# Moving the small softmax-sum transfers from SyncE's queue to ScalarE's, with other due times in the planner that orders an attention stage

## The chip, the cores and the metric

The kernel runs on one core of a Trainium2 chip. The metric is the device time of one execution in microseconds, as the median of several runs.

## The reference

Three blocks follow each other, all in 32-bit floats. q is averaged over pairs of rows first.

```python
# attention: 4 batches, 8 heads, 1152 keys, 576 pooled queries, head size 64
q_pool = q.reshape(B, H, S // 2, 2, D).mean(axis=3)
scores = scale * np.matmul(q_pool, k.transpose(0, 1, 3, 2))
scores = scores - np.max(scores, axis=-1, keepdims=True)
attn = np.exp(scores)
attn = attn / (np.sum(attn, axis=-1, keepdims=True) + 1e-09)
x = np.matmul(attn, v)                  # -> 2304 tokens x 512
# soft mixture of experts: 8 experts, 4 slots each, 512 -> 1024 -> 512
logits = x @ phi                        # softmax over tokens (d) and over slots (c)
slot_input = d.T @ x
slot_out[e] = np.maximum(slot_input[e] @ w1[e], 0.0) @ w2[e]
y = c @ slot_out
# gated block, 512 -> 2048 -> 512
h = y @ w_in
out = (h * np.cos(h)) @ w_out
```

## The kernel before

**The attention stage** works on 16 pairs of heads. A pair has two halves (`a`) of 288 queries, and a half has nine key tiles (`t`) of 128 keys. For each key tile `scores` (L457, L460) makes a 128x576 block on TensorE in PSUM, `exps` (L468) turns it into `E` on ScalarE, `e_sum` (L479, L481) adds `E` into a running sum `ES` on GpSimd, and `av` (L487) multiplies `E` by V on TensorE into a sum of its own in PSUM. `av` splits TensorE's array by columns, while scores split it by rows; the planner calls these modes "c64" and "r64".

Ahead of a half, `max_pair` (L412, TensorE) and `max_pair_red` (L421, VectorE) find the maxima that the scores are shifted by: 9 such blocks for the first half, 6 for the second. Scores, maxima, transposes and the spread sums share three PSUM slots (`take="2"`): a slot is free again only when ScalarE or VectorE has read it. `E` has five buffers.

After a pair, `fin` closes it: `sum4` adds `ES` over partitions (L508), `sum4_copy` moves it to SBUF, **`sum4_turn`** (L520) sends 4.5 KB by DMA into a layout of 128 partitions (`rt`), `sum4_rec` takes reciprocals as a high and a low part (`hl`, L548 to L551), **`sum4_back`** (L557) sends the two parts back by two DMAs (`rh`), `sum4_spread` (L565) broadcasts them on TensorE, and `pair_mul` (L570) multiplies.

Beside this, 32 pieces of w_in and w_out are converted (`conv_load` to `conv_store`: ScalarE L289 and L294, VectorE L298, L301 and L307, GpSimd L313) and stored to DRAM, and expert weights are loaded ahead into buffers as they come free (`late_piece`, `held_piece`, L251). The tiles `raw` and `cvt` of the conversion are two such buffers, which take two pieces of 256 KB each once the last conversion is done.

**The planner** `in_order` sets the order of all this. Each operation has an engine, an assumed time, what it depends on, a PSUM or `E` slot and a due time; the planner walks through an assumed time line and takes, per engine, the operation with the earliest due time among those that can start. A change of TensorE's mode counts as 2.5 us of due time. Each engine then runs its list strictly in that order. `GROUPS` says which key tiles' `av` form one operation; `PAIR`, `MAX_BEG`, `AV_DUE` and the 13.6 in `convert` set due times.

**The last pair** (p = 15) is finished in finer steps: `fin_sum` (L530), `rec_mul` (L541 to L577), `l_x` (L793), `l_mm` (L782), `l_max`, `l_exp`, `l_weigh`. The first half's are planned too; the second half's are written out behind the planner's list, beginning with an `l_mm`, `l_eT` (L744) and a `fin_sum`.

**Behind attention** come the experts (L1175, L1208), which read 128 weight pieces of 256 KB, then the converted weights are loaded back (L1251 to L1259), and then the gated block (L1343, L1379, L1381) runs to the end.

Of the kernel before, what the change touches and what calls it, by code (L numbers as in the profile page):

```python
# [45 lines left out]
LAT = {"PE": 0.27, "ACT": 0.1, "DVE": 0.1, "POOL": 0.12, "SP": 0.0}  # L46
# [1 line left out]
KB_US = 250.0  # L48
PAIR = 26
FIRST_AT = 22.0  # L50
MAX_BEG, MAX_MID, MAX_END = 4, 6, 4
AV_DUE = 6
GROUPS = ((0, 1), (2, 3), (4, 5), (6, 7, 8))
LAST_GROUPS = ((0, 1), (2, 3), (4, 5), (6, 7))


class Op:


    def __init__(self, steps, fn, deps=(), due=0.0, take=None, mode=None, port=False, kb=None, at=0.0):  # L60
        self.steps, self.fn, self.deps = steps, fn, [d for d in deps if d is not None]
        self.due, self.take, self.mode, self.port, self.kb, self.at = due, take, mode, port, kb, at
        self.after, self.users, self.of = [], 0, []
        self.end = None

# [8 lines left out]
def in_order(ops, room):  # L74

    left = {}
    for o in ops:
        left[o] = len(o.deps)
        for d in o.deps:
            d.after.append(o)  # L80
    ready = [o for o in ops if not left[o]]
    free = {e: 0.0 for e in ("PE", "ACT", "DVE", "POOL", "SP")}
    spots = {k: [(0.0, i) for i in range(n)] for k, n in room.items()}
    mode, done, until, wire = None, 0, {}, 0.0
    while ready:
        best = {}
        for o in ready:
            e = o.steps[0][0]
            t = max(free[e], o.at, max((d.end + (1.0 if e == "SP" else 0.0) if d.steps[-1][0] != e or d.kb else d.end - LAT[e] for d in o.deps), default=0.0))
            if o.take:  # L90
                if not spots[o.take]:
                    continue
                t = max(t, min(spots[o.take])[0])
            if o.port:
                t = max(t, free["POOL" if e == "DVE" else "DVE"] if until.get("POOL" if e == "DVE" else "DVE") else 0.0)
            best.setdefault(e, []).append((t, o))
        pick = None
        for e, c in best.items():
            t0 = min(t for t, _ in c)
            near = [(o.due + (2.5 if o.mode and o.mode != mode else 0.0) + 0 * (t - t0), t, o) for t, o in c if t <= t0 + 0.1]  # L100
            due, t, o = min(near, key=lambda x: x[0])
            if pick is None or t < pick[0]:
                pick = t, o
        t, o = pick
        ready.remove(o)
        spot = None
        if o.take:
            spot = min(spots[o.take])
            spots[o.take].remove(spot)
            o.spot, o.free_at = spot[1], 0.0  # L110
        for e, dur in o.steps:
            t = max(t, free[e])
            if e == "PE" and o.mode != mode:
                t += SWITCH[o.mode]
                mode = o.mode
            free[e] = t + dur
            until[e] = o.port
            t = t + dur + LAT[e]
        if o.kb is not None:

            wire = max(wire, t) + o.kb / KB_US
            t = wire + 2.5
        o.end = t
        o.fn(o)
        done += 1
        if o.take and not o.users:
            spots[o.take].append((o.end, o.spot))
        for x in o.of:
            x.users -= 1
            x.free_at = max(x.free_at, o.end)  # L130
            if not x.users:
                spots[x.take].append((x.free_at, x.spot))
        for a in o.after:
            left[a] -= 1
            if not left[a]:
                ready.append(a)
    assert done == len(ops), (done, len(ops))
# [3 lines left out]
def kernel(  # L141
# [12 lines left out]
    nc = tc.nc  # L154
# [6 lines left out]
    NP = B * H // 2  # L161
# [339 lines left out]
    fs = {}  # L501
# [15 lines left out]

    def sum4_turn(p):
        rt = sm.tile([128, HF // 32], FP32, tag="rt", name="rt")
        nc.sync.dma_start(out=rt, in_=fs.pop("r").rearrange("(r x) (j c) -> r x j c", x=32, j=32)[:, 0])  # L520
        fs["rt"] = rt


# [30 lines left out]
    def sum4_back(p):  # L554
        hl = fs.pop("hl")
        for i in range(2):
            nc.sync.dma_start(  # L557
                out=rh[4 * i:4 * i + 4].bitcast(FP32).rearrange("r (j c) -> r j c", j=32), in_=hl[:, i].bitcast(FP32)
            )

# [246 lines left out]
    def due_at(p, a=0, t=0):  # L807
        return FIRST_AT + (p + (a * NJ + t) / (2 * NJ)) * PAIR

    def attention():  # L810
        ops = []

        def add(steps, f, *args, **kw):
            def fn(o):
                cur[0] = o
                f(*args)

            o = Op([steps] if isinstance(steps[0], str) else steps, fn, **kw)
            ops.append(o)
            return o  # L820
# [69 lines left out]
                    out_[p, a] = add(("ACT", .32), av_out, p, a, deps=[avo[p, a, NJ - 1], mul.get(p - 2)], due=due_at(p, a, 10)).uses(first)  # L890

        def fin(p):
            z = due_at(p + 1)
            s4[p] = m = add(("PE", .5), sum4, p, deps=[es[p, 0, NJ - 1], es[p, 1, NJ - 1], spread.get(p - 1)], due=z + 4, take="1", mode="c32")
            c = add(("ACT", .31), sum4_copy, p, deps=[m], due=z + 5).uses(m)
            c = add(("SP", .6), sum4_turn, p, deps=[c], due=z + 5.2, kb=50)
            c = add([("DVE", .13), ("ACT", .12), ("DVE", .12)], sum4_rec, p, deps=[c], due=z + 9)
            c = add(("SP", 1.2), sum4_back, p, deps=[c], due=z + 10, kb=100)
            spread[p] = m = add(("PE", .55), sum4_spread, p, deps=[c], due=z + 14, take="2", mode="r64")
            b = (p - HP - 1) // HP  # L900
            mul[p] = add(("DVE", .66), pair_mul, p, deps=[m, out_[p, 1], bl.get(b), *[bx.get((b, g)) for g in range(5)]], due=z + 15).uses(m)
            if p % HP == HP - 1 and p < NP - 1:
                b = p // HP
                bl[b] = add([("PE", 1.2), ("DVE", .5), ("ACT", .4), ("DVE", .4)], b_logits, b, deps=[mul[p], bp1.get(b - 1)], due=z + 19, take="1", mode="c32")
                for g in range(5):
                    bx[b, g] = add([("PE", .45), ("ACT", .55)], b_x, b, g, deps=[mul[p], bp1.get(b - 1)], due=z + 20 + 3 * g, take="2", mode="r64")
                e = add([("PE", .27), ("ACT", .35)], b_e, b, deps=[bl[b]], due=z + 24, take="1", mode="full")
                bp0[b] = add(
                    [("PE", .9), ("DVE", .1), ("ACT", .2), ("DVE", 1.5)], b_part, b, 0, deps=[e, *[bx[b, g] for g in range(4)]],
                    due=z + 34, take="1", mode="c32",  # L910
                )
                bp1[b] = add([("PE", .9), ("ACT", .55)], b_part, b, 1, deps=[bp0[b], bx[b, 4]], due=z + 36, take="1", mode="c32")

        def convert(i):
            z = FIRST_AT + 8 + i * 13.6
            if i and i - 1 not in cu:
                return
            l = add(("SP", .6), conv_load, i, deps=[cu[i - 1]["sign"]] if i else (), due=z - 9, kb=512, at=z - 12)
            x = add(("ACT", .62), conv_act, i, deps=[l, cu[i - 1]["store"] if i else None], due=z)
            y = add(("ACT", .62), conv_low, i, deps=[x], due=z + .5)  # L920
            m = add(("DVE", .8), conv_mag, i, deps=[x], due=z + 2, port=True)
            s = add(("DVE", .65), conv_sign, i, deps=[m], due=z + 3, port=True)
            r = add(("POOL", 1.25), conv_round, i, deps=[s, y], due=z + 5, port=True)
            cu[i] = dict(sign=s, store=add(("SP", .5), conv_store, i, deps=[r], due=z + 6, kb=256))
# [13 lines left out]
        for i in range(RING):  # L938
            z = due_at(3.4 + i * 8 / 36)
# [4 lines left out]
        p, b = NP - 1, B - 2  # L944

        def d(t):
            return due_at(p, 1, t)

        def maxima():
            for i in range(3):  # L950
# [43 lines left out]
        c = add(("DVE", .35), lambda: l_max(lt[0], 0), deps=[m], due=d(6.5)).uses(m)  # L994
        c = add([("DVE", .1), ("ACT", .75)], lambda: l_exp(lt[0], 0), deps=[c], due=d(7)).uses(m)
# [4 lines left out]
    with tc.manual_schedule():  # L1000
# [8 lines left out]
        for h in range(2):  # L1009
# [6 lines left out]
            out=pick, in0=idn[0:64, 0:4].rearrange("p (r o) -> p r o", o=1).to_broadcast([64, 4, 64]),  # L1016
# [3 lines left out]
            out=sel.rearrange("p (s o) -> p s o", o=1), in_=idn.rearrange("p (g s) -> p s g", g=4), axis=AX.X, op=ALU.add  # L1020
# [9 lines left out]
        p = NP - 1  # L1030
# [40 lines left out]
        for kk in range(HP):  # L1071
            nc.tensor.matmul(
                out=pm[:, kk * NS:(kk + 1) * NS], lhsT=part[0][:, kk * 128:(kk + 1) * 128], rhs=sel, start=True, stop=True
# [96 lines left out]
        for g in range(NG):  # L1170
            h1p = [ps_m.tile([128, 512], FP32, tag=f"h{a}", name=f"h{a}") for a in range(2)]
            for kk in range(HP):
                for a in range(2):
                    for e in range(4):
                        nc.tensor.matmul(  # L1175
                            out=h1p[a][32 * e:32 * e + 32, :], lhsT=slT[:, kk, :], rhs=pieces[used + e],
# [298 lines left out]
```

## Time and profile before

| what | us |
|---|---|
| three runs | 836.56 median (834.33 to 836.94) |
| the profiled execution | 832.92, of it 831.1 span from first to last instruction |
| attention's pairs until the last exponential | about 0 to 521.7 of the span |
| the rest of attention's list and the last pair's close | 521.7 to 549.6 |
| experts | 549.6 to 594.3 |
| gated block with its start | 594.3 to 831.1 |

The last four rows are marked off by instructions in the trace: the last `exps` ends near 521.7, the first expert matmul starts at 549.6, the last one's sum is done by 594.3. The profiled execution lies 3.6 us under the median of the three runs.

### The profile page before, as it was taken

The page shows a single profiled execution, that of the slowest core. Times are in us where ns is not written, and L with a number is a line of the kernel's source. Part 1 is how long each engine was busy: PE and PEld are TensorE (multiplying, and loading weights), DVE is VectorE, ACT ScalarE, POOL GpSimd, SP SyncE. Part 2 cuts the span into 40 slices and gives each one's busy share as a digit, 9 for nine tenths or more (in the row PEclk, how much of TensorE's full clock was granted, in tenths as well). Part 3 has the DMA queues.
Part 4 walks back from the last instruction along what each step waited for, and adds up shares of the span by engine and source line. Part 5 has one row for each costly group of instructions (what it writes and reads, how often), then busy time and mean ns, then how long its engine had stood idle before and what let it go on. Part 6 is the DMA issues. An engine that isn't in the chain of part 4 may idle for free.

```text
span 831.1 us, 16390 instructions
## 1 busy us (share of the span) xinstructions
PE 776.5 (93%) x6336; PEld 531.1 (64%) x6336; DVE 555.2 (67%) x828; ACT 448.7 (54%) x837; POOL 536.2 (65%) x415
## 2 busy tenths in 40 slices
PE   4999999999999999989999999699999999999997
PEld 2766666666666666556665656333467888888886
DVE  6777877777877767868876775522276756666662
ACT  1565556465555564555665655223376766666662
POOL 1698889787798877878876979411375544444442
PEclk9999999999999999999999999999999999999999
DMA  8432553553634654443515314299951000000001
GB/s 201 122 96 69 148 137 128 141 167 124 161 116 113 190 156 147 126 144 107 126 42 158 130 58 141 97 328 386 386 205 26 26 5 22 27 26 26 26 26 26
DMA packets 86482, 101.48 MB, mean 122 GB/s; under 512 B 48260, under 2 KB 48260, under 8 KB 86404
## 3 DMA queue, kind: packets, MB, share of 16 engines
q1 hardware_dynamic: 86324, 100.30, 40.2%
q8 instruction: 50, 0.82, 0.4%
q14 instruction: 28, 0.23, 0.1%
q10 hardware_dynamic: 80, 0.13, 0.0%
HBM read 87.10 MB, written 13.11 MB: 121 GB/s over the span
## 4 chain that ended last, share of the span: by engine, by line
PE 69%; DVE 16%; ACT 6%; issue 4%; POOL 3%; DMA 1%; ACTq 0%; SPq 0%; POOLq 0%; DVEq 0%
PE o L1379 15%; PE av L487 13%; PE mx L457 11%; PE o L1381 7%; DVE nm L421 6%; PE mx L412 5%; PE mx L460 3%; POOL ES L481 2%; PE po L1208 2%; ACT E L468 2%; PE h L1175 2%; DVE cvt L298 2%; PE u L1343 2%; DVE cvt L301 2%; DVE cvt L307 2%
## 5 line engine op out<-in xcount | busy, mean ns | idle before, releaser
L481 POOL TENSOR_TENSOR ES<-ES,E 128x576 f32<-128x576 f32 x223 | 325.9, 1462 | 45.0 <-ACT E L468 31.4
L421 DVE TENSOR_REDUCE nm<-mx 128x2 f32<-128x768 f32 x240 | 223.8, 953 | 81.2 <-PE mx L412 80.2
L468 ACT ACTIVATE E<-mx 128x576 f32<-128x576 f32 x288 | 179.5, 650 | 145.5 <-PE mx L460 126.9
L457 PE MATMUL mx<-Q,kX 64*128 64x288 f32 x1152 | 178.8, 322 | 14.1 <-DVE nm L421 9.8
L487 PE MATMUL av<-E,vn 128*64 128x288 f32 x1152 | 169.8, 421 | 0.0
L1363 POOL TENSOR_TENSOR lo<-g,hi 128x512 fp32r<-128x512 f32 (+1 forms) x73 | 94.2, 1291 | 110.5 <-DVE hi L1361 105.8
L457 PEld LDWEIGHTS mx<-Q,kX 64*128 64x128 f32 x1152 | 111.0, 186 | 66.0 <-DVE nm L421 25.6
L1379 PE MATMUL o<-w_hi,hi 128*128 128x512 f32 x288 | 113.2, 393 | 0.7 <-DVE hi L1361 0.7
L1381 PE MATMUL o<-w_lo,hi 128*128 128x512 f32 x288 | 113.2, 393 | 0.3 <-DVE w_lo L1267 0.3
L487 PEld LDWEIGHTS av<-E,vn 128*64 128x64 f32 x1152 | 72.2, 137 | 55.7 <-issue 23.0
L412 PE MATMUL mx<-kX,Q 64*128 64x384 f32 x480 | 92.4, 403 | 9.7 <-DVE nm L421 4.4
L457 PE MATMUL mx<-Q,kY 64*128 64x288 f32 x576 | 87.7, 294 | 0.0
L460 PE MATMUL mx<-NM,one_row 64*128 64x288 f32 x576 | 87.4, 293 | 0.0
L1379 PE MATMUL o<-w_hi,lo 128*128 128x512 f32 x288 | 77.4, 389 | 0.0
L479 POOL TENSOR_TENSOR ES<-E 128x576 f32<-128x576 f32 x31 | 45.8, 1477 | 46.1 <-ACT E L468 46.1
L1348 ACT ACTIVATE t<-u 128x512 f32<-128x512 f32 (+1 forms) x73 | 43.0, 591 | 58.0 <-PE u L1343 58.0
L1350 DVE SCALAR_TENSOR_TENSOR r<-t,u 128x512 f32<-128x512 f32 (+1 forms) x73 | 49.4, 679 | 36.4 <-ACT t L1348 35.8
L1359 DVE SCALAR_TENSOR_TENSOR g<-r,u 128x512 f32<-128x512 f32 (+1 forms) x73 | 49.6, 680 | 35.4 <-ACT r L1357 35.4
L412 PEld LDWEIGHTS mx<-kX,Q 64*128 64x128 f32 x480 | 45.5, 191 | 38.6 <-DVE nm L421 15.0
L313 POOL TENSOR_TENSOR cvt<-cvt 128x512 uint32<-128x512 uint32 x32 | 44.2, 1381 | 31.7 <-DVE cvt L307 16.6
L1379 PEld LDWEIGHTS o<-w_hi,lo 128*128 128x128 f32 x288 | 54.1, 188 | 11.4
L1379 PEld LDWEIGHTS o<-w_hi,hi 128*128 128x128 f32 x288 | 54.2, 188 | 10.9 <-DVE hi L1361 0.9
(223 smaller groups left out, 1007.0 us busy)
## 6 DMA issues: line engine op xcount, KB each, us to landing
w<-in_moe_w_dram SPq DMA_DIRECT2D x89, 256.0 KB
qn<-in_q_dram SPq DMA_DIRECT2D x16, 576.0 KB
kn<-in_k_dram SPq DMA_DIRECT2D x16, 576.0 KB
vn<-in_v_dram SPq DMA_DIRECT2D x16, 576.0 KB
raw<-in_moe_w_in_dram SPq DMA_DIRECT2D x16, 512.0 KB
w<-cvt SPq DMA_DIRECT2D x32, 256.0 KB
raw<-in_moe_w_out_dram SPq DMA_DIRECT2D x16, 512.0 KB
lw<-in_moe_w_dram SPq DMA_DIRECT2D x29, 256.0 KB
```

What stands on the lines that cost most here:

```text
L412: nc.tensor.matmul(out=m[:, h, 0:384], lhsT=Q1[p % 2][hs, AT[i]:AT[i] + 128], rhs=X[p][hs, ks], start=True, stop=True)
L421: nc.vector.tensor_reduce(out=nm3[p][:, i, :, c:c + 1], in_=m[:, :, 0:384], axis=AX.X, op=ALU.max)
L457: nc.tensor.matmul(out=sc[:, h, 0:HF], lhsT=x[hs, ks], rhs=y[hs, qs], start=(n == 0), stop=False)
L460: nc.tensor.matmul(out=sc[:, h, 0:HF], lhsT=one_row[hs, :], rhs=NM[p % 2][hs, qs], start=False, stop=True)
L468: nc.scalar.activation(out=e, in_=sc[:, :, 0:HF], func=AF.Exp, scale=1.0 / 16.0)
L481: nc.gpsimd.tensor_tensor(out=ES[p, a], in0=ES[p, a], in1=E[p, a, t], op=ALU.add)
L487: nc.tensor.matmul(out=av_t[p, a][64 * h:64 * h + 64, 0:HF], lhsT=vn[p][:, h, t, :], rhs=E[p, a, t][:, h, :], start=(t == 0), stop=(t == N ...
L1350: nc.vector.scalar_tensor_tensor(out=r, in0=t, scalar=MAGIC, in1=u, op0=ALU.subtract, op1=ALU.subtract)
L1359: nc.vector.scalar_tensor_tensor(out=g, in0=r, scalar=1.0, in1=u, op0=ALU.subtract, op1=ALU.mult)
L1363: nc.gpsimd.tensor_tensor(out=lo[:, 0:n], in0=g, in1=hi[:, 0:n].bitcast(FP32), op=ALU.subtract)
L1379: nc.tensor.matmul(out=o, lhsT=x, rhs=w_hi[ff], start=(ff == 0 and not part), stop=bool(part and ff == NF - 1))
L1381: nc.tensor.matmul(out=o, lhsT=x, rhs=w_lo[ff], start=False, stop=False)
```

## The change

`sum4_turn` and `sum4_back` are issued in ScalarE's queue instead of SyncE's. The planner counts ScalarE as taken for 0.65 and 1.2 us by them, and the data as landed 2.8 us later (`land`). Each key tile's `av` is an operation of its own, due 5.1 us behind its scores instead of 8.7 (`AV_DUE` times 26/18). The conversions are due every 11.5 us instead of 13.6. The first half's maxima become due 6 us later (`MAX_BEG` 4 to 10). `fin` of pair 14 and the planned close of pair 15 are due 8 us sooner (`SOON`). Among operations that start within 0.1 us of each other, a later start now counts five times against the due time.

```diff
-MAX_BEG, MAX_MID, MAX_END = 4, 6, 4
-AV_DUE = 6
-GROUPS = ((0, 1), (2, 3), (4, 5), (6, 7, 8))
-LAST_GROUPS = ((0, 1), (2, 3), (4, 5), (6, 7))
+MAX_BEG, MAX_MID, MAX_END = 10, 6, 4
+AV_DUE = 3.5
+CONV, SOON = 11.5, 8
+GROUPS = tuple((i,) for i in range(9))
+LAST_GROUPS = GROUPS[:8]
...
-            near = [(o.due + (2.5 if o.mode and o.mode != mode else 0.0) + 0 * (t - t0), t, o) for t, o in c if t <= t0 + 0.1]
+            near = [(o.due + (2.5 if o.mode and o.mode != mode else 0.0) + 5 * (t - t0), t, o) for t, o in c if t <= t0 + 0.1]
...
-        o.end = t
+        o.end = t + o.land
...
-        nc.sync.dma_start(out=rt, in_=fs.pop("r").rearrange("(r x) (j c) -> r x j c", x=32, j=32)[:, 0])
+        nc.scalar.dma_start(out=rt, in_=fs.pop("r").rearrange("(r x) (j c) -> r x j c", x=32, j=32)[:, 0])
...
-            nc.sync.dma_start(
+            nc.scalar.dma_start(
...
-            z = due_at(p + 1)
+            z = due_at(p + 1) - (SOON if p == NP - 2 else 0)
...
-            c = add(("SP", .6), sum4_turn, p, deps=[c], due=z + 5.2, kb=50)
+            c = add(("ACT", .65), sum4_turn, p, deps=[c], due=z + 5.2, land=2.8)
...
-            c = add(("SP", 1.2), sum4_back, p, deps=[c], due=z + 10, kb=100)
+            c = add(("ACT", 1.2), sum4_back, p, deps=[c], due=z + 10, land=2.8)
...
-            z = FIRST_AT + 8 + i * 13.6
+            z = FIRST_AT + 8 + i * CONV
...
-            return due_at(p, 1, t)
+            return due_at(p, 1, t) - SOON
```

What the change moves is seen at three places. A new line near the top shifts all later line numbers by one.

TensorE, second half of pair 7, from its fifth key tile on; L487/L488 is `av`, where x4 is two key tiles and x2 is one (two heads each). Before:

```order
L457 MATMUL mx<-Q_1_110,kX 128x288 x2
L457 MATMUL mx<-Q_1_110,kY 128x288 x2
L457 MATMUL mx<-Q_1_112,kX 128x288 x2
L460 MATMUL mx<-NM_114,one_row 128x288 x2
L412 MATMUL mx<-kX,Q_0_109 128x384 x2
L487 MATMUL av<-E,vn 64x288 x4
L565 MATMUL mx<-rh,pick 128x288 x2
```

After, about the same place:

```order
L461 MATMUL mx<-NM_114,one_row 128x288 x2
L488 MATMUL av<-E,vn 64x288 x2
L413 MATMUL mx<-kX,Q_0_109 128x384 x2
...
L461 MATMUL mx<-NM_114,one_row 128x288 x2
L413 MATMUL mx<-kX,Q_0_109 128x384 x2
L488 MATMUL av<-E,vn 64x288 x2
L413 MATMUL mx<-kX,Q_0_109 128x384 x2
L488 MATMUL av<-E,vn 64x288 x2
```

Where the old list has one run of two key tiles, the new one often has a run of a single tile, with a maximum between two of them. Over the whole program the list has 127 runs of `av` before (93 of two tiles, 31 of three, 3 of other lengths up to five) and 174 after (85 of one tile, 73 of two, 9 of three, 5 of four, 2 of five).

TensorE, the end of the planner's list, where L793 is `l_x`, L782 `l_mm`, L565 the spread of pair 14's sums and L457/L460 the last scores. Before:

```order
L460 MATMUL mx<-NM_114,one_row 128x288 x2
L487 MATMUL av<-E,vn 64x288 x4
L565 MATMUL mx<-rh,pick 128x288 x2
L487 MATMUL av<-E,vn 64x288 x8
L793 MATMUL mx<-idn,xT 96x128 x8
L782 MATMUL mx<-xT,phi_sb 32x288 x4
L793 MATMUL mx<-idn,xT 96x128 x4
L729 MATMUL mx<-nM_124,gsel 128x1
L782 MATMUL mx<-xT,phi_sb 32x288
L744 MATMUL mx<-idn,e_7217 96x32 x3
```

After (the spread stands further ahead, at the start of the second half):

```order
L488 MATMUL av<-E,vn 64x288 x10
L794 MATMUL mx<-idn,xT 96x128 x4
...
L783 MATMUL mx<-xT,phi_sb 32x288 x4
L794 MATMUL mx<-idn,xT 96x128 x4
...
L461 MATMUL mx<-NM_114,one_row 128x288 x2
L794 MATMUL mx<-idn,xT 96x128 x4
L488 MATMUL av<-E,vn 64x288 x2
L730 MATMUL mx<-nM_124,gsel 128x1
L488 MATMUL av<-E,vn 64x288 x4
L783 MATMUL mx<-xT,phi_sb 32x288
L745 MATMUL mx<-idn,e_7215 96x32 x3
```

Before, the spread, two `l_x` and the `l_mm` of four products, the third `l_x` and six tiles of `av` stood behind the last scores; now one `l_x` and three tiles of `av` do.

SyncE's queue at the same place, where L317 is the store of a converted piece, lw the pieces that go into freed buffers (nine of them into kX, kY, vn, Q1, Q2 and NM), hw others of that kind. Before:

```order
L282 DMA raw<-in_moe_w_out_dram 128x1024
...
L317 DMA w_31_160<-cvt 128x512
L251 DMA lw<-in_moe_w_dram 128x512 x11
L251 DMA hw<-in_moe_w_dram 128x512 x8
L251 DMA w<-in_moe_w_dram 128x512 x49
L1251 DMA win_q<-w_0_129 128x512
```

After:

```order
L252 DMA hw<-in_moe_w_dram 128x512 x2
L252 DMA lw<-in_moe_w_dram 128x512 x9
L252 DMA hw<-in_moe_w_dram 128x512 x8
L252 DMA w<-in_moe_w_dram 128x512 x49
L1252 DMA win_q<-w_0_129 128x512
```

The last four conversions have left the end of the list. Counted by the scores ahead of them, conversion 31 stood behind the last scores and now stands in the middle of pair 14, and the four pieces for `raw` and `cvt` are issued there too.

## Rows read from the trace of the kernel before

**Rows 1.** Stretch: length, busy of PE, PEld, DVE, ACT, POOL, clock, DMA share, GB/s.

```profile
24.20:500.40 476.20, 451.09 (x4548) 298.93 (x4548) 361.65 (x471) 269.20 (x499) 387.68 (x268) 0.99 0.45 127
...
521.70:549.60 27.90, 19.11 (x130) 9.64 (x126) 16.21 (x39) 8.27 (x21) 7.13 (x6) 0.94 0.41 133
549.60:594.30 44.70, 44.30 (x300) 13.22 (x300) 8.85 (x46) 10.35 (x32) 9.58 (x29) 1.00 1.05 386
594.30:612.90 18.60, 16.95 (x104) 11.69 (x104) 10.12 (x20) 13.15 (x29) 10.45 (x9) 1.00 1.05 386
```

**Rows 2.** The same view for two pair periods (first exponential to the next pair's).

```profile
239.40:268.20 28.80, 28.38 (x287) 19.25 (x287) 20.75 (x29) 17.11 (x32) 25.05 (x18) 1.00 0.57 155
335.00:368.30 33.30, 29.06 (x285) 18.93 (x284) 27.01 (x31) 16.98 (x31) 28.53 (x21) 1.00 0.45 121
```

**Rows 3.** Waits from 24.2 to 500.4: total us, times, longest.

```profile
ACT E L468 <- PE mx L460: 122.7, 128, 2.9
...
PEld mx L457 <- DVE nm L421: 25.6, 43, 2.5
...
PE mx L457 <- DVE nm L421: 9.8, 16, 2.2
```

**Rows 4.** TensorE's timeline in pair 2, around one run of `av`.

```profile
72.43 0.34 PE L412 MATMUL mx<-kX,Q 64*128 64x384 f32 x2
72.70 1.19 PE L487 MATMUL av<-E,vn 128*64 128x288 f32 x8
73.83 0.40 PE L457 MATMUL mx<-Q,kX 64*128 64x288 f32 x2
74.06 0.29 PE L457 MATMUL mx<-Q,kY 64*128 64x288 f32 x2
74.19 0.29 PE L457 MATMUL mx<-Q,kX 64*128 64x288 f32 x2
...
74.46 0.33 PE L412 MATMUL mx<-kX,Q 64*128 64x384 f32 x2
74.63 0.29 PE L457 MATMUL mx<-Q,kX 64*128 64x288 f32 x2
```

**Rows 5.** The chain that ended last: `av` of two and three tiles.

```profile
34.42 1.12 PE av L487 x8
38.23 1.61 PE av L487 x12
```

**Rows 6.** The small transfer `rt` around pair 1's beginning: ns min/median/max, start.

```profile
L520 SPq DMA_DIRECT2D rt<-rec x1: 705/705/705, 57.3 to 57.3; - x1
L548 DVE RECIPROCAL rt<-rt x1: 205/205/205, 61.5 to 61.5; 128x9 f32<-128x9 f32 x1
...
  DVE rt L548: 0.9, 1
```

**Rows 7.** The issues of `rh` on SyncE, ns min/median/max.

```profile
L557 SPq DMA_DIRECT2D rh<-hl x30: 547/580/1177, 61.9 to 514.2; - x30
```

**Rows 8.** TensorE's timeline from the last scores to the last pair's close.

```profile
515.77 0.71 PE L530 MATMUL mx<-ES,ones 128*64 128x288 f32 x4 [1.92 <-POOL ES L481]
...
519.49 0.29 PE L460 MATMUL mx<-NM,one_row 64*128 64x288 f32 x2
...
529.11 1.09 PE L793 MATMUL mx<-idn,xT 128*96 128x128 f32 x4 [5.20 <-DVE xT L577]
...
530.74 2.99 PE L782 MATMUL mx<-xT,phi_sb 128*32 128x288 f32 x8
533.66 0.64 PE L793 MATMUL mx<-idn,xT 128*96 128x128 f32 x4
...
536.84 0.67 PE L782 MATMUL mx<-xT,phi_sb 128*32 128x288 f32 x2
```

**Rows 9.** SyncE's queue there: start, us, issue.

```profile
543.50 5.49 SPq L251 DMA_DIRECT2D lw<-in_moe_w_dram  x11
```

**Rows 10.** Busy times just ahead of the experts, columns as in rows 1.

```profile
543.00:549.60 6.60, 6.05 (x59) 3.50 (x59) 1.99 (x9) 3.12 (x9) 0.00 (x0) 1.00 0.79 244
```

More of the change, by code (lines that the diff above doesn't have):

```diff
@@ L50, with __init__ @@
 FIRST_AT = 22.0
-MAX_BEG, MAX_MID, MAX_END = 4, 6, 4
-AV_DUE = 6
-GROUPS = ((0, 1), (2, 3), (4, 5), (6, 7, 8))
-LAST_GROUPS = ((0, 1), (2, 3), (4, 5), (6, 7))
+MAX_BEG, MAX_MID, MAX_END = 10, 6, 4
[3 more added lines that the diff above has]
+LAST_GROUPS = GROUPS[:8]
 class Op:
-    def __init__(self, steps, fn, deps=(), due=0.0, take=None, mode=None, port=False, kb=None, at=0.0):
+    def __init__(self, steps, fn, deps=(), due=0.0, take=None, mode=None, port=False, kb=None, land=0.0, at=0.0):
         self.steps, self.fn, self.deps = steps, fn, [d for d in deps if d is not None]
-        self.due, self.take, self.mode, self.port, self.kb, self.at = due, take, mode, port, kb, at
+        self.due, self.take, self.mode, self.port, self.kb, self.land, self.at = due, take, mode, port, kb, land, at
         self.after, self.users, self.of = [], 0, []
@@ L88, in in_order @@
             e = o.steps[0][0]
-            t = max(free[e], o.at, max((d.end + (1.0 if e == "SP" else 0.0) if d.steps[-1][0] != e or d.kb else d.end - LAT[e] for d in o.deps), default=0.0))
+            t = max(free[e], o.at, max((d.end + (1.0 if e == "SP" else 0.0) if d.steps[-1][0] != e or d.kb or d.land else d.end - LAT[e] for d in o.deps), default=0.0))
             if o.take:
```

## The prediction

> **What bounds the kernel now.** I read the busy times by stretch first [rows 1]. Attention's pairs take 476 of 831 us, and TensorE is busy in 451 of them; but matmuls overlap, so this share hides short stalls. No other engine is near: GpSimd 388, VectorE 362, ScalarE 269 us. Behind the pairs stands a stretch of 27.9 us with TensorE busy in only 19.1. The experts' stretch and the one behind it run at 386 GB/s with the DMA share full: there the weights set the pace. What follows them holds nothing that the change touches.
>
> Then I compared pair periods [rows 2]. The same TensorE instructions (287 and 285 matmul records) take 28.8 us in one pair and 33.3 in another. In the slow one VectorE works 27.0 us instead of 20.8. So a pair is not TensorE's sum of work alone: some 4 us of a slow one are stalls. The waits say which [rows 3]: TensorE waits for VectorE's reduction of the maxima (`nm`), at the scores 9.8 us at matmuls and 25.6 us at weight loads, 35.4 in all, part of which the matmul before still covers. The cause is the three shared PSUM slots: while VectorE is at a conversion or a sum of q, maxima wait in their slots, and the next scores find none.
>
> **The change part by part.**
>
> *More runs of `av`.* The printed order has 174 runs instead of 127, 47 more. What one costs is read from the timeline [rows 4]. Without a run, a maximum's start is followed by the next scores 0.17 us later (74.46 to 74.63), and within scores starts are 0.13 apart (74.06 to 74.19). With one, `av` starts 0.27 behind the maximum (72.43 to 72.70), and the first two matmul groups of the scores behind it are 0.23 apart (73.83 to 74.06): 0.10 lost going in, 0.10 coming out. In the chain a run of two tiles takes 1.12 us and one of three 1.61 [rows 5], so a tile is 0.49 and a run has a fixed 0.14. That is 0.34 a run, and 47 x 0.34 = **16.0 us more on TensorE**. It stands on the path wherever TensorE is the bound. Bounds: 0, if each new run fell into a stall, and 16.0; I take all of it here, and count stalls apart.
>
> *Maxima later, conversions denser, `av` sooner.* The first half's nine maxima were due over 18 us and overlapped the second half's six; now they are due over 12 us behind them, which leaves VectorE free for the next pair's q and k work at a pair's start. A conversion is due every 11.5 instead of 13.6 us, which puts 2.3 instead of 1.9 of them into a pair of 26 planned us: more work for VectorE in a pair, but spread differently, and none in the last one and a half pairs. What this gives back no row shows. Below, it is nothing, or a loss if the crowd of maxima is worse. Above, it is 35.4 us. The good pair of rows 2 shows that a list of this kind can run nearly free of stalls, and the slow one loses 4.5. I take a third of the bound, **12 us less**, which is nearly three slow pairs turned into good ones.
>
> *The small transfers.* On SyncE an issue of `rh` took 0.58 us in the median [rows 7], and `rt` makes 15 like it beside the 30: 45 x 0.58 = 26.1 us that now stand in ScalarE's list. ScalarE is busy 269 of 476 us [rows 1] and waits 122.7 us for scores [rows 3]; these waits are the cover, so I cost it at nothing. Without the cover it is 26 us. What lands too late is next: `rt`, issued from 57.3 to 58.0, let VectorE go on at 61.5 after a wait of 0.9 [rows 6], 3.5 us behind the issue's end, and the planner now counts 2.8. If ScalarE's queue is no quicker, VectorE stands 0.7 us for each pair, 15 x 0.7 = 10.5 us, most of it in VectorE's idle time; I take **2 us more**, between 0 and 10.5. The Trainium skill (DMA: Bandwidth & Descriptors, section "Issuing engines are not separate DMA queues") says that transfers started by several engines run on the same 16 DMA engines, and that another issuer saves only the sequencer's issue time. By that rule the landing gets no quicker and VectorE's 0.7 us a pair would stay; no run here shows it yet.
>
> *The last pair.* From the last scores' end (519.49 + 0.29) to the first matmul of the close (536.84) 17.1 us pass, with TensorE standing 5.20 us of them for VectorE [rows 8], which does conversion 30 ahead of the products that TensorE needs. In the new order only one `l_x` (0.64) and three tiles of `av` (3 x 0.49 + 0.34) stand behind the last scores, 2.5 us, and two exponentials have to end: I take 3.5. What moved ahead is the `l_mm` (2.99), two `l_x` (1.28), the spread, which has about as many columns as an `l_x` (576 to 512) and is put at the same 0.64, and three tiles (1.47): 6.4 us, of which 1.9 fit into the stall at 515.77. So 17.1 - 3.5 - 4.5 = **9.1 us less**; between 4, if the steps of the chain wait for each other in their new places too, and 13, if all that moved finds idle time.
>
> *The weights.* Eleven pieces (2.88 MB) were issued only from 543.50 on [rows 9], behind the last conversion's store in the queue. By 549.6 the queues had moved 6.6 us x 244 GB/s = 1.61 MB [rows 10], so 1.27 MB were still ahead of the experts' stream, 3.3 us at 386 GB/s. Now four pieces land a pair earlier, and the other nine wait for no store. The stream is DMA-bound, so I take **3.3 us less**; between 0 and 7.5 (all 2.88 MB).
>
> **The sum.** 832.9 + 16.0 - 12 + 2 - 9.1 - 3.3 = 826.5 for the profiled execution, 6.4 us less. That execution lies 3.6 us under the runs' median, so against the median it is 836.6 - 6.4 = **830.2**.
>
> **The rivals.**
>
> *TensorE becomes the bound and nothing comes back* (the other side). The runs' 16.0 us stay, the 12 don't come. The time is 836.6 + 16.0 + 2 - 12.4 = 842.2. For it: TensorE is the busiest engine in rows 1, and the new order adds to it alone. Against it: the slow pairs' stalls are there to be filled. It decides at the amount given back: with less than 3 us the kernel is slower by over 0.3% (2.5 us, about what a measurement of this kernel can tell from no change), with 3 to 8 the same, with more faster.
>
> *ScalarE's issues are not covered.* If a third of the 26 us keeps exponentials waiting while all three slots hold scores, that is 8.7 more: 838.9. All of it would give 856. It turns the forecast over when more than 9 us of the 26 come through. For it: ScalarE hands back the slots. Against it: the 122.7 us of waiting.
>
> *Stalls nearly vanish.* With 30 of the 35.4 us back the time is 836.6 - 6.4 - 18 = 812.2. For it: the good pair in rows 2. Against it: GpSimd, with 25.1 us busy in that pair's 28.8, would hold the pairs above some 27 us, and batches' ends add work to two of four pairs.
>
> *The small transfers do nothing*, since VectorE was never late by them: that changes 2 us and no sign.
>
> **Chances.** The forecast, with 8 to 22 us given back, 0.42. Nearly no stalls 0.18, also faster. Three to 8 us given back, the same, 0.12. Nothing given back 0.14 and ScalarE's issues exposed 0.14, both slower. So 0.60 faster, 0.12 the same, 0.28 slower. The range of 8 in 10 reaches towards both ends, 813 to 847; the forecast's own is 820 to 834.
>
> **What would show it.** In the changed profile, TensorE's pair periods should be near 30 us with fewer of 33; the scores' waits for `nm` should be some 12 us fewer over the pairs; `av` as x4 records should take 0.63 us in the chain. From the last scores to the close's `l_mm` should pass some 3.5 instead of 17.1 us, with no conversion behind pair 14; and the stretch from the first expert matmul to the end of the 386 GB/s should be 60 instead of 63.3 us. The forecast is wrong if ScalarE stands long at its DMA issues with TensorE waiting for E, if the scores' waits for VectorE stay near 35 us, or if the last pair's chain, due sooner, makes TensorE stand among its last scores instead of behind them.

## The result and the profile after

The changed kernel takes **829.47 us** in the median of eleven runs (824.68 to 837.93), the kernel before 836.90 in eleven runs beside them (834.33 to 839.99). The ratio is 0.9913 (95%: 0.9888 to 0.9939): 0.9% faster. The forecast was 830.2, with a range of 813 to 847.

The profiled execution of after took 824.68 us (span 822.9) and is the lowest of its eleven, 4.8 us under their median; that of before lies 3.6 under the median beside which the forecast was made. The two spans differ by 8.2 us. Line numbers of after are one higher.

The busy times by stretch, in the columns of [rows 1]; the second row is the rest of the list and the close behind the last exponential:

```profile
24.20:500.40 476.20, 448.48 (x4469) 290.48 (x4467) 365.26 (x473) 270.83 (x498) 386.26 (x267) 0.99 0.47 133
533.70:546.70 13.00, 12.40 (x101) 6.61 (x100) 5.67 (x19) 4.47 (x13) 0.29 (x1) 1.00 0.76 260
546.70:591.50 44.80, 43.70 (x330) 15.75 (x330) 9.80 (x48) 13.24 (x39) 10.45 (x30) 1.00 1.03 375
591.50:605.80 14.30, 13.33 (x78) 8.82 (x78) 9.99 (x20) 10.68 (x23) 9.97 (x10) 1.00 1.03 377
```

The reader should see two things. The first row looks like that of [rows 1]: shares of busy time tell nothing of what changed among the pairs. But the 27.9 us of [rows 1] in which TensorE worked only 19.1 have become 13.0 with 12.4 at work.

The waits from 24.2 to 500.4, which answer to [rows 3] (total us, times, longest):

```profile
ACT hl L551 <- DVE rt L549: 18.9, 11, 3.8
PEld mx L413 <- DVE nm L422: 13.9, 18, 2.5
PEld mx L458 <- DVE nm L422: 12.3, 24, 1.3
...
DVE rt L549 <- DMA rt<-rec: 8.9, 6, 3.5
...
PEld av L488 <- ACT E L469: 7.0, 7, 2.6
...
PE mx L413 <- DVE nm L422: 6.4, 7, 2.0
...
PE mx L458 <- DVE nm L422: 4.3, 7, 1.2
...
PE av L488 <- ACT E L469: 3.8, 3, 2.1
```

Three more lines of the same view of the kernel before:

```profile
PEld mx L412 <- DVE nm L421: 9.6, 21, 1.0
...
ACT hl L550 <- DVE rt L548: 5.2, 8, 0.9
...
PE mx L412 <- DVE nm L421: 1.9, 4, 0.8
```

The scores' waits for the maxima fell from 35.4 to 16.6 us. The maxima's own waits (L412, now L413) for a slot rose from 11.5 (9.6 at weight loads, 1.9 at matmuls) to 20.3, so 10.0 us of both went. Three waits in a row grew: VectorE for the landing of `rt`, which it had not waited for before, ScalarE for VectorE's reciprocal, 18.9 us where it was 5.2, and `av` for an `E` that ScalarE makes late. What this looks like in pair 1 is in the timelines of ScalarE, VectorE and TensorE (start, us, what, idle before):

```profile
57.86 1.25 ACTq L521 DMA_DIRECT2D rt<-rec  x1
...
63.97 0.21 ACT L551 ACTIVATE hl<-rt 128x9 fp32r<-128x9 f32 x1 [3.77 <-DVE rt L549]
64.08 0.63 ACT L469 ACTIVATE E<-mx 128x576 f32<-128x576 f32 x1
```
```profile
63.72 0.22 DVE L549 RECIPROCAL rt<-rt 128x9 f32<-128x9 f32 x1 [3.48 <-DMA rt<-rec]
```
```profile
64.77 0.71 PE L488 MATMUL av<-E,vn 128*64 128x288 f32 x4 [2.11 <-ACT E L469]
```

ScalarE has `hl` next in its list and stands 3.77 us for it, with an exponential queued behind; TensorE's `av` wants that `E` and stands 2.11.

TensorE's timeline from the last scores on, which answers to [rows 8], and SyncE's queue, which answers to [rows 9]:

```profile
526.96 0.64 PE L794 MATMUL mx<-idn,xT 128*96 128x128 f32 x4
...
528.26 2.13 PE L783 MATMUL mx<-xT,phi_sb 128*32 128x288 f32 x8
530.32 0.64 PE L794 MATMUL mx<-idn,xT 128*96 128x128 f32 x4
...
531.92 0.29 PE L461 MATMUL mx<-NM,one_row 64*128 64x288 f32 x2
532.14 0.64 PE L794 MATMUL mx<-idn,xT 128*96 128x128 f32 x4
532.71 0.71 PE L488 MATMUL av<-E,vn 128*64 128x288 f32 x4
533.35 0.38 PE L730 MATMUL mx<-nM,gsel 32*128 32x1 f32 x2
533.66 1.19 PE L488 MATMUL av<-E,vn 128*64 128x288 f32 x8
534.78 0.67 PE L783 MATMUL mx<-xT,phi_sb 128*32 128x288 f32 x2
```
```profile
532.12 7.46 SPq L252 DMA_DIRECT2D lw<-in_moe_w_dram  x9
539.67 5.57 SPq L252 DMA_DIRECT2D hw<-in_moe_w_dram  x8
```

The eight products of `l_mm` and two `l_x` now stand ahead of the last scores, and the close's `l_mm` (534.78) follows them without an idle row. The nine pieces are issued at 532.12 instead of 543.50, because the last conversion, at 539.6 on GpSimd before, is at 491.8.

Where the 8.2 us came from, between these marks: the last scores end 12.4 us later (519.78, now 532.21), of which 7.6 lie in the 15 pair periods (first exponentials from 24.20 to 500.36, now from 24.01 to 507.74) and 5.0 in the last pair; from there to the close's `l_mm` 2.57 instead of 17.06, so 14.5 less; from it to the first expert matmul 11.9 instead of 12.8; from there to the end of the full DMA stretch (605.8) 59.1 instead of 63.3, so 4.2 less; behind it 1.1 less.

### The profile page after: what moved, and what is told of

It reads as the page before. It is cut to its first block, busy times and chain, and to the rows that moved or that the text cites. A ratio compares the mean times of both kernels' runs of the same rounds, so it can differ in the third digit from the quotient of the medians.

```text
span 822.9 us, 16379 instructions
## 1 busy us (share of the span) xinstructions
PE 776.1 (94%) x6336; PEld 526.8 (64%) x6336; DVE 556.7 (68%) x828; ACT 450.7 (55%) x837; POOL 535.5 (65%) x415
## 4 chain that ended last, share of the span: by engine, by line
PE 70%; DVE 16%; DMA 4%; ACT 4%; issue 3%; POOL 2%; ACTq 0%; SPq 0%; DVEq 0%; POOLq 0%
PE o L1380 15%; PE av L488 12%; PE mx L458 12%; PE o L1382 7%; PE mx L413 5%; DVE nm L422 5%; PE mx L461 3%; DMA rt<-rec 2%; PE po L1209 2%; POOL ES L482 2%; PE u L1344 2%; PE h L1176 2%; DVE cvt L299 2%; DVE cvt L302 2%; DVE cvt L308 2%
## 5 line engine op out<-in xcount | busy, mean ns | idle before, releaser
L469 ACT ACTIVATE E<-mx 128x576 f32<-128x576 f32 x288 | 183.4, 649 | 141.2 <-PE mx L461 122.1
L458 PE MATMUL mx<-Q,kX 64*128 64x288 f32 x1152 | 182.0, 326 | 6.7 <-DVE nm L422 4.3
L488 PE MATMUL av<-E,vn 128*64 128x288 f32 x1152 | 180.7, 425 | 4.0 <-ACT E L469 3.8
L413 PE MATMUL mx<-kX,Q 64*128 64x384 f32 x480 | 94.3, 400 | 13.8 <-DVE nm L422 8.8
L488 PEld LDWEIGHTS av<-E,vn 128*64 128x64 f32 x1152 | 67.2, 136 | 59.9 <-issue 29.9
L413 PEld LDWEIGHTS mx<-kX,Q 64*128 64x128 f32 x480 | 46.6, 191 | 47.8 <-DVE nm L422 19.3
L1360 DVE SCALAR_TENSOR_TENSOR g<-r,u 128x512 f32<-128x512 f32 (+1 forms) x73 | 49.6, 679 | 35.4 <-ACT r L1358 35.3
L1380 PEld LDWEIGHTS o<-w_hi,lo 128*128 128x128 f32 x288 | 54.0, 188 | 11.5
L1382 PEld LDWEIGHTS o<-w_lo,hi 128*128 128x128 f32 x288 | 54.2, 188 | 10.2 <-DVE w_lo L1268 0.6
```

The lines of the kernel that those rows point to most:

```text
L413: nc.tensor.matmul(out=m[:, h, 0:384], lhsT=Q1[p % 2][hs, AT[i]:AT[i] + 128], rhs=X[p][hs, ks], start=True, stop=True)
L458: nc.tensor.matmul(out=sc[:, h, 0:HF], lhsT=x[hs, ks], rhs=y[hs, qs], start=(n == 0), stop=False)
L469: nc.scalar.activation(out=e, in_=sc[:, :, 0:HF], func=AF.Exp, scale=1.0 / 16.0)
L488: nc.tensor.matmul(out=av_t[p, a][64 * h:64 * h + 64, 0:HF], lhsT=vn[p][:, h, t, :], rhs=E[p, a, t][:, h, :], start=(t == 0), stop=(t == N ...
L1360: nc.vector.scalar_tensor_tensor(out=g, in0=r, scalar=1.0, in1=u, op0=ALU.subtract, op1=ALU.mult)
L1380: nc.tensor.matmul(out=o, lhsT=x, rhs=w_hi[ff], start=(ff == 0 and not part), stop=bool(part and ff == NF - 1))
```

## The experiments

All ratios are against the kernel before in the same series (its medians: 836.72 for the first four runs, 835.69 for the next four, 836.51 for the last four).

### Only the queue taken back

```diff
-        nc.scalar.dma_start(out=rt, in_=fs.pop("r").rearrange("(r x) (j c) -> r x j c", x=32, j=32)[:, 0])
+        nc.sync.dma_start(out=rt, in_=fs.pop("r").rearrange("(r x) (j c) -> r x j c", x=32, j=32)[:, 0])
...
-            nc.scalar.dma_start(
+            nc.sync.dma_start(
```

Every engine's order stays as changed; only the small transfers leave ScalarE's queue for SyncE's.

> The changed kernel with every engine's order kept as it is, but the rt and rh transfers issued in SyncE's queue, at the places that the list gives them. Theory (the queue does nothing by itself; the landing is as late in either, and ScalarE's issues are covered): 827 to 832 us, as the changed kernel's 829.5, with VectorE's waits for rt within 3 us of its 8.9. Rival (in SyncE's queue the small transfers stand behind loads that wait for buffers): 835 to 850, VectorE's waits for rt over 20 us. Second rival (ScalarE's issues did cost): 820 to 825.

823.30 us (819.21 to 823.96), ratio 0.9825 (0.9805 to 0.9844): 6.2 us below the changed kernel, and **the best version of all**. Its waits:

```profile
ACT hl L551 <- DVE rt L549: 14.6, 11, 3.3
...
DVE rt L549 <- DMA rt<-rec: 3.7, 2, 2.2
...
PEld av L488 <- ACT E L469: 3.5, 3, 1.4
...
PE av L488 <- ACT E L469: 1.9, 3, 0.9
```

All four are smaller than in the changed kernel, so the theory fell and the second rival held. At pair 1's start `rt` was issued at 57.8 and used at 62.1; from ScalarE's queue it was issued at 57.86 and used at 63.72. So ScalarE's queue brought it no sooner. The rule of the Trainium skill that the prediction weighed (DMA: Bandwidth & Descriptors, "Issuing engines are not separate DMA queues") agrees with this.

It even brought it later, and SyncE's queue shows why. First the changed kernel, then this run:

```profile
57.72 0.61 SPq L335 DMA_DIRECT2D kn<-in_k_dram  x1
```
```profile
57.81 0.70 SPq L521 DMA_DIRECT2D rt<-rec  x1
58.56 0.62 SPq L335 DMA_DIRECT2D kn<-in_k_dram  x1
```

In SyncE's list `rt` stands ahead of `kn`, a load of 576 KB, and holds it back; moved to ScalarE's queue it no longer does, and `kn` is issued first. Of the 15 pairs this happens in eight, each time with one load of 256 to 576 KB. In these eight, by the traces' DMA packets, the last packet of `rt` ends 3.77 us in the mean behind the beginning of its issue from ScalarE's queue and 2.42 from SyncE's; in the other seven it is 2.20 and 2.17. All 8.9 us that VectorE waits for the landing in the changed kernel fall into six of the eight. The two profiled executions are only 0.8 us apart, one the lowest of its runs and the other next to the highest, so where the 6.2 us of the medians lie can't be read from the two traces alone.

The same swap on the order of before:

```diff
-        nc.sync.dma_start(out=rt, in_=fs.pop("r").rearrange("(r x) (j c) -> r x j c", x=32, j=32)[:, 0])
+        nc.scalar.dma_start(out=rt, in_=fs.pop("r").rearrange("(r x) (j c) -> r x j c", x=32, j=32)[:, 0])
...
-            nc.sync.dma_start(
+            nc.scalar.dma_start(
```

> The kernel before with every engine's order kept as it is, but rt and rh issued in ScalarE's queue, at the places that the list gives them. Theory (issues on ScalarE hold up exponentials, as the 6 us between the changed kernel and its run with SyncE's queue say): 839 to 845 us against some 836.7. Rival (only the changed kernel's tight due times made it so; here the list leaves the transfers 7 to 10 us): 835 to 838.

838.34, ratio 1.0034 (1.0015 to 1.0054), 2.7 us slower. So the move by itself costs in either order, 2.7 and 6.2 us; here a little less than the theory had. From 24.2 to 500.4 VectorE waits for the landing only 0.8 us in this run, so the 2.7 hardly come from it.

### The planned landing later

```diff
-            c = add(("ACT", .65), sum4_turn, p, deps=[c], due=z + 5.2, land=2.8)
+            c = add(("ACT", .65), sum4_turn, p, deps=[c], due=z + 5.2, land=4.5)
-            c = add(("ACT", 1.2), sum4_back, p, deps=[c], due=z + 10, land=2.8)
+            c = add(("ACT", 1.2), sum4_back, p, deps=[c], due=z + 10, land=4.5)
```

> The changed kernel with the landing of rt and rh counted as 4.5 us instead of 2.8 in the planner, near what the trace shows. Theory (late rt makes VectorE and ScalarE stand, 8.9 and 19.5 us in the trace, and about a third of this reaches TensorE): those waits fall under 5 us each, and the time falls by 3 to 9, to 820 to 826. Rival (these waits lie beside TensorE's work): 828 to 831 with the waits gone.

833.11, ratio 0.9954 (0.9934 to 0.9974). The theory fell:

```profile
ACT hl L551 <- DVE rt L549: 18.9, 8, 5.0
...
DVE rt L549 <- DMA rt<-rec: 9.9, 5, 4.1
```

The waits are as long as ever, and the new list also put two `l_x` and the `l_mm` of eight products behind the last scores again: 8.7 us instead of 3.2 from their end to `l_eT`. Why the waits stayed isn't settled.

### The groups of `av`

The changed kernel with the old groups (128 runs of `av`) and their old due time:

```diff
-AV_DUE = 3.5
-GROUPS = tuple((i,) for i in range(9))
+AV_DUE = 6
+GROUPS = ((0, 1), (2, 3), (4, 5), (6, 7, 8))
...
```

> The changed kernel with av in groups of two and three key tiles and the due time of before: 128 runs of av instead of 174. Theory (a run costs 0.34 us on TensorE and TensorE is the bound in the pairs): 46 x 0.34 = 15.6 us less work, of which half or more is gained, 814 to 822. Rival (sooner single tiles free E and spread the work, and the runs fall into stalls): 829 to 838.

840.59, ratio 1.0048 (1.0023 to 1.0073), 11 us above the changed kernel, and so outside the theory and above its rival. VectorE's waits for the landing of `rt` (24.2 to 500.4) are 17.2 us in this list instead of 8.9, so part of the 11 can be theirs. The reverse, single tiles due sooner in the kernel before (176 runs):

```diff
-AV_DUE = 6
-GROUPS = ((0, 1), (2, 3), (4, 5), (6, 7, 8))
+AV_DUE = 3.5
+GROUPS = tuple((i,) for i in range(9))
...
```

> The kernel before with av in groups of one key tile, due 5.1 us behind the scores, and nothing else of the change. 49 more runs of av by the order. Theory of the prediction (0.34 us each on a TensorE that is the bound): 840 to 853. Rival (as the changed kernel with the old groups was 11 us slower, single tiles give back more than their runs cost): 824 to 834.

830.65, ratio 0.9944 (0.9925 to 0.9964): 5.0 us less, with 49 more runs. Its last scores end at 519.0, where they ended at 519.78 with 127 runs. So 49 more runs didn't lengthen this list's pairs; whether they cost less, or the new list gives back what they cost, this run can't part.

To price a run without changing any order, the kernel before got a product of 2 columns, into two unused columns of PSUM and in the scores' mode, between the tiles of each `av` operation, 159 in all:

```diff
+                                    if x != g[0]:
+                                        nc.tensor.matmul(
+                                            out=av_t[p, a][:, 300:302], lhsT=one_row[0:64, :], rhs=one_row[0:64, 0:2],
+                                            start=False, stop=False,
+                                        )
```

> The kernel before in its own order, with a product of two columns in the scores' row mode put between the tiles of each group of av, into columns of av's PSUM bank that nothing reads: 159 more runs of av, with nothing else moved. Theory (0.34 us a run and some 0.06 for the small product, all on the path): 159 x 0.40 = 64 us more, 895 to 905. Rival (half of the runs' cost falls into stalls, which then shrink): 860 to 875. Rival (runs cost next to nothing): under 850.

863.63, ratio 1.0335 (1.0313 to 1.0357): 27.9 us for 159 runs, 0.176 each. This is about half of the 0.34 by rows, although in the timeline a split run costs just what the rows said:

```profile
75.66 0.71 PE L487 MATMUL av<-E,vn 128*64 128x288 f32 x4
76.29 0.27 PE L882 MATMUL av<-one_row 64*128 64x2 f32 x1
76.49 0.71 PE L487 MATMUL av<-E,vn 128*64 128x288 f32 x4
77.12 0.40 PE L457 MATMUL mx<-Q,kX 64*128 64x288 f32 x2
```

From `av` to the next scores pass 1.46 us; unsplit, in [rows 4], 1.13 (72.70 to 73.83): 0.33 more, the small product included. For 159 that is 52.5, of which 24.6 never reached the end. The waits from 24.2 to 536 show where they went:

```profile
PEld mx L457 <- DVE nm L421: 13.5, 29, 0.8
...
PEld mx L412 <- DVE nm L421: 4.0, 10, 0.8
...
PE mx L457 <- DVE nm L421: 2.3, 6, 0.5
```

The scores' waits for maxima are 15.8 us where they were 35.4, and the maxima's at weight loads 4.0 where they were 9.6 (before, up to 519.8, both sums are the same as up to 500.4): 25.2 less, near the 24.6. A slower TensorE gives VectorE the time that it was waited for.

### The maxima's due time

```diff
-MAX_BEG, MAX_MID, MAX_END = 10, 6, 4
+MAX_BEG, MAX_MID, MAX_END = 4, 6, 4
```

> The changed kernel with the first half's maxima due from 4 us on again (MAX_BEG 4 for 10). Theory (crowded early maxima make TensorE wait for VectorE; the later due times gave some 10 us back): 836 to 845, with waits of scores and maxima for nm up by 10 us or more. Rival (the later due times do nothing): 826 to 833.

842.41, ratio 1.0078 (1.0057 to 1.0099), 13 us above the changed kernel. The scores' waits from 24.2 to 500.4 are 41.6 us, where the changed kernel has 16.6:

```profile
PEld mx L458 <- DVE nm L422: 29.1, 41, 3.5
PE mx L458 <- DVE nm L422: 12.5, 16, 3.0
```

### The conversions' pace and the last pair

The changed kernel with both taken back:

```diff
-CONV, SOON = 11.5, 8
+CONV, SOON = 13.6, 0
```

> The changed kernel with conversions due every 13.6 us again and the last pair's operations not sooner (0 instead of 8 us). Theory (the gain is in the last pair and the weights behind it): 9.1 + 3.3 us or more come back, 840 to 848, above the kernel before. Rival (the gain is in the pairs' new order): 828 to 834.

853.46, ratio 1.0193 (1.0176 to 1.0209), 24 us above the changed kernel and past the theory's 848. The last conversion is on GpSimd at 560.5, the last scores end at 547.0, the first expert matmul starts at 572.7. The landing of `rt` is 6.8% of its chain of waits, some 58 us, and 2.4% of that of the changed kernel, some 20:

```profile
by line: PE o L1380 14.2%; PE av L488 10.9%; PE mx L458 10.4%; PE o L1382 7.1%; DMA rt<-rec 6.8%; DVE nm L422 6.1%; PE mx L413 4.6%; issue 3.2%; PE mx L461 2.7%; PE po L1209 2.3%; PE h L1176 1.9%; PE u L1344 1.7%; DVE cvt L299 1.7%; DVE cvt
```
```profile
by line: PE o L1380 14.7%; PE av L488 12.4%; PE mx L458 11.9%; PE o L1382 7.4%; PE mx L413 5.2%; DVE nm L422 5.2%; issue 3.2%; PE mx L461 3.2%; DMA rt<-rec 2.4%; PE po L1209 2.2%; POOL ES L482 1.8%; PE u L1344 1.8%; PE h L1176 1.8%; DVE cvt
```

With `SOON` alone taken back and the pace kept:

```diff
-CONV, SOON = 11.5, 8
+CONV, SOON = 11.5, 0
```

> The changed kernel with the last pair's operations not due sooner (SOON 0 for 8), conversions still every 11.5 us. Theory (the conversions' pace is most of the last pair's gain, since it takes conversion 28 to 31 and their store out of the end): 830 to 838. Rival (the sooner due times are most of it): 842 to 854.

831.22, ratio 0.9932 (0.9905 to 0.9959). So the pace carries 22 of the 24 us, not `SOON`. But 12 of the 22 lie in the 15 pair periods (500.1 us with the old pace, 487.8 with the new one), where VectorE's waits for the landing of `rt` are 24.3 and 11.4 us; the runs don't price the last pair alone. Both edits alone on the kernel before:

```diff
-            z = due_at(p + 1)
+            z = due_at(p + 1) - (8 if p == NP - 2 else 0)
...
-            z = FIRST_AT + 8 + i * 13.6
+            z = FIRST_AT + 8 + i * 11.5
...
-            return due_at(p, 1, t)
+            return due_at(p, 1, t) - 8
```

> The kernel before with the conversions due every 11.5 us and the last pair's operations due 8 us sooner, and nothing else of the change. Theory (the gain is the last pair and the weights behind it): 12 to 24 us less, 813 to 825. Rival (denser conversions cost the pairs what the end gains): 830 to 838.

835.82, ratio 1.0002 (0.9987 to 1.0017): nothing. From the last scores to the close's `l_mm` pass 9.3 instead of 17.1 us, but the last scores end at 537.2, 17 us later. TensorE's timeline there:

```profile
536.90 0.30 PE L460 MATMUL mx<-NM,one_row 64*128 64x288 f32 x2
537.13 3.13 PE L487 MATMUL av<-E,vn 128*64 128x288 f32 x24
540.19 1.08 PE L793 MATMUL mx<-idn,xT 128*96 128x128 f32 x8
541.20 2.13 PE L782 MATMUL mx<-xT,phi_sb 128*32 128x288 f32 x8
...
546.19 0.38 PE L729 MATMUL mx<-nM,gsel 32*128 32x1 f32 x2 [2.29 <-ACT lgr L723]
546.50 0.67 PE L782 MATMUL mx<-xT,phi_sb 128*32 128x288 f32 x2
```

With `av` in big groups the products still stand behind the last scores, and the 2.29 us of waiting for ScalarE's copy `lgr`, in whose place the changed kernel has scores and `av`, stay open.

### Another list, and a list as a control

The changed kernel, its small transfers on SyncE and planned there:

```diff
-            c = add(("ACT", .65), sum4_turn, p, deps=[c], due=z + 5.2, land=2.8)
+            c = add(("SP", .6), sum4_turn, p, deps=[c], due=z + 5.2, kb=50)
-            c = add(("ACT", 1.2), sum4_back, p, deps=[c], due=z + 10, land=2.8)
+            c = add(("SP", 1.2), sum4_back, p, deps=[c], due=z + 10, kb=100)
```

> The changed kernel with the small transfers issued by SyncE and planned so, as before; all due times of the change stay, and the list is made anew from them. Theory (the move to ScalarE costs some 6 us in this order): 821 to 826. Rival (what counts is which list comes out, and this one has two products' transposes behind the last scores again): 829 to 838.

830.61, ratio 0.9932 (0.9911 to 0.9954). Its last scores end at 527.5, 3.4 us sooner than with the queue alone taken back, but `l_eT` starts 8.9 us behind them instead of 3.2. And a change that means nothing and only makes another list:

```diff
-AV_DUE = 3.5
+AV_DUE = 3.7
```

> The changed kernel with av due 5.3 instead of 5.1 us behind its scores (AV_DUE 3.7 for 3.5): a change of no meaning, which only makes the planner's choices fall out otherwise. Theory (single due times matter little, so the differences between the other runs have causes): 826 to 833. Rival (any new list moves the time by 5 us or more, so that differences of that size between lists say nothing of the part that was changed): below 824 or above 835.

830.95, ratio 0.9939 (0.9917 to 0.9961), 1.5 us above the changed kernel. But the run before it and the best version share their edits and differ by 7 us in their lists alone. So of the runs that planned anew, I take only differences of 11 us and more as told apart (old groups, maxima, pace). That bound is a choice that two comparisons don't prove, and the old groups stand just at it. The three that kept their engines' order need no such allowance.

## Why the prediction was right

Sign and size held: 830.2 forecast, 829.47 measured; 826.5 for the profiled execution, 824.68 measured. It came out of terms of which some were off, up and down, so that the total lies as near as it does is partly luck.

**The pairs.** Forecast were 10.5 us more until the last scores' end (16.0 - 12 + 2, and 4.5 of work moved ahead); 12.4 were found: 7.6 in the pair periods, where 6.0 were forecast, and 5.0 in the last pair, where 4.5 were. The sum held, but the terms of its 6.0 didn't:

- *"47 x 0.34 = 16.0 us more on TensorE ... I take all of it here, and count stalls apart"* is the step that was mis-sized. The 0.34 is right for one run in the trace (0.33), but what reaches the end is 0.176, so some 8 us (47 x 0.176, an estimate from the run with added products). The prediction took a run's price and the stalls as two independent terms; the split runs show them to be one, since a longer TensorE shortens the same waits.
- *"12 us less"* for the spread isn't confirmed as a size. 10.0 us of waits for maxima went, counting those of the scores and of the maxima, but a longer TensorE takes some of these away by itself, as the split runs show. With 8 for the runs and 6.2 for the queue, the 7.6 found leave about 7 given back, an estimate by difference; taking back the maxima's due time in the changed kernel costs 13 (842.41 against 829.47). Either speaks against the rival "nothing comes back", whose 842.2 didn't come.
- *"2 us more"* for the small transfers was too little: 6.2, between the 2 and the 8.7 of the rival that ScalarE's issues are not covered. The prediction misread [rows 6] here. The 0.9 us there are ScalarE's wait at `hl` for VectorE's reciprocal; VectorE itself came to it straight from two maxima, without a wait, and the last packet of `rt` had ended at 59.3:

```profile
59.73 1.82 DVE L421 TENSOR_REDUCE nm<-mx 128x2 f32<-128x768 f32 x2 [0.52 <-PE mx L412]
61.47 0.20 DVE L548 RECIPROCAL rt<-rt 128x9 f32<-128x9 f32 x1
```

So the 3.5 us were no landing time, and no row stands behind the 0.7 a pair and the bound of 10.5; that VectorE's 8.9 us of waiting lie inside that bound is luck. What the step left out is the place in the queue: taken out of SyncE's list, `rt` lets a large load go first in eight of 15 pairs. The rival of the uncovered issues named the right engine but not this act. The issues themselves take what the prediction said (0.58 us in the median for `rt`). With the queue taken back, ScalarE's standing at `hl` falls from 18.9 to 14.6 us, VectorE's waits for the landing from 8.9 to 3.7, and those of `av` for a late `E` from 10.8 to 5.4. That most of the 6.2 us come from this chain is argued from these waits; no run parted it from the issues' own time, and the 2.7 us in the order of before, nearly without waits for the landing, speak for a share of something else.

- *Pair periods "near 30 us"* didn't come. From first exponential to first exponential, as in [rows 2], the 15 periods are 31.7 us in the mean before and 32.2 after, and five instead of four are above 33, one of them 38.5.

**The last pair.** 3.5 us instead of 17.1 were forecast from the last scores to the close's `l_mm`, and 2.57 measured; no conversion stands there. In the trace the chain of waits from 491.6 to the experts holds TensorE and little else. The prediction gave the whole term to the edits of the last pair and the pace. The experiments add that these edits alone give nothing (835.82), since the last scores then end 17 us later, which eats what is gained behind them. Which of the other edits they need isn't shown; without the single tiles of `av` (840.59) or the later maxima (842.41) the rest of the change is slower than the kernel before.

**The weights.** 3.3 us were forecast for the stretch from the first expert matmul to the end of the full DMA, 4.2 measured (63.3 to 59.1), with 376 instead of 386 GB/s.

Left open: how the 6.2 us of the queue divide, why a later planned landing took no wait away, and what the fivefold weight on a later start does, which wasn't tried alone.

## What to carry to other kernels

Price a queue by swapping it with every engine's order kept: here the one edit that looked free cost 6.2 us, and leaving it out gives the best version (823.3 us). See also what the moved transfer held back in the queue that it leaves. A price read from a timeline is a price on one engine; where that engine waits for another one, add the cost to the kernel on purpose and see how much arrives. Parts of a list can't be added up: the same due times gave nothing in one setting and 24 us in another, so try an edit in both, and run a meaningless new list beside it to see what luck is worth.

## What the runs showed of the hardware

A change of TensorE's mode for 2 columns between two `av` tiles costs 0.33 us in the timeline, the small product included. Where the move to ScalarE's queue let a load of 256 to 576 KB from SyncE's be issued ahead of a transfer of 4.5 KB, that transfer's last packet ended 1.35 us later in the mean (3.77 against 2.42 us behind the beginning of its issue); where no load passed it, the queue made no difference (2.20 against 2.17).
